# Zero products, a bias add and a float32 inverse in the opening phase of a Fourier and MoE kernel

## The chip, the cores and the metric

The kernel runs on one core of a Trainium2 chip. The metric is the device time of one execution in microseconds (us). The core has five engines that each run their own list of instructions: PE (TensorE, matrix products into the banks of PSUM), DVE (VectorE), ACT (ScalarE), POOL (GpSimd) and SP (SyncE, which here only issues transfers). Transfers (DMAs) are issued from the queues of SP, ACT and POOL. An instruction that waits holds up all that stands behind it on its engine, and the order on each engine is fixed when the program is built: a planner goes through the program in the order in which it is written, weighs it with its own table of costs, and writes one list for each engine.

## The reference

```python
B, S, D, FF = 8, 3008, 256, 2048
X = np.fft.rfft(x, axis=1)                 # x: [8, 3008, 256]
Yr = X.real @ w_r - X.imag @ w_i + b_r     # complex 256x256 product on each bin
Yi = X.real @ w_i + X.imag @ w_r + b_i
Yr, Yi = shrink(Yr, 0.01), shrink(Yi, 0.01)   # sign(y) * max(|y| - 0.01, 0)
y = np.fft.irfft(Yr + 1j * Yi, n=3008, axis=1)
h = np.maximum(y.reshape(24064, 256) @ w_in, 0.0)   # w_in: [256, 2048], float64
out = (h * h) @ w_out                               # w_out: [2048, 256], float64
```

## The kernel before

A Fourier transform of length 3008 = 64 x 47 is done in two stages of matrix products with constant matrices, forward and back. Between them lies the complex product on each bin, the bias and the shrinking. The result goes into the MoE part: two large products with a squared Relu between, which is most of the work.

The 8 batches run one behind the other, and the forward and inverse Fourier work of a later batch is woven into the MoE steps of an earlier one, by jobs with due times in half steps (`jobs`, L755 to L791). The first batch has nothing to be woven into. So the kernel opens with a *front* phase of its own (L653 to L731), with its own SBUF tiles and all eight PSUM banks, and then a *main* phase.

**The ring.** `Fwd32` (L370 to L392) is the first Fourier stage of batch 0. Seven loads of x (tag `big`, four buffers) come in on SP's queue. DVE folds each into a sum and a difference (L380, tag `small`, four buffers), PE multiplies them with `am32` (L384), ACT evicts to `xe` (L391), SP's queue stores to the scratch tensor `s1`. In the loop at L666 the load of a later x is issued ahead of a tile's product, and both ahead of the store of the one before. At the start `load_bias` (L128) loads the bias and a selector matrix on ACT's queue, into two of the four `small` buffers; ACT and DVE turn them into `bb` and `one`.

**Second-batch tiles.** `Fwd2` (L348) is the same stage for the thirteen tiles of batch 1, with four float32 products each instead of folds. With `PRE, FILL = 10, 3`, three of them run after the ring, seven after the units, and the last three in the main phase. In the front their evictions go to tag `xf`, two buffers, and their stores to POOL's queue.

**The units.** `Unit32` (L405 to L452) takes one of the 24 groups of bins of batch 0 through the second Fourier stage (`fwd`, L422), a sign change (`bins`, L428), the product with the weights (`mix`: one product `one` x `bb` for the bias at L433, then four with `w32` at L437), the shrinking (`shrink`: ACT's Relu from the bank at L442, DVE's minimum at L443) and the first inverse stage (`back`, L449). `store_back` (L252) splits the result into a high and a low part (`kuh` by ACT, `kul` by DVE) and stores both to the scratch `s3` on SP's queue. The loop at L703 runs `fwd` and `bins` for unit r+1, `shrink` for r-1, `back` and the store for r-2, and `mix` for r. The matrices of four units at a time (`kbb`, `kk`) are loaded by `load_group`, behind the store of an earlier unit.

**The weights.** The MoE weights come as float64, in 16 parts. `convert` (L689) puts a part together from its two 32-bit halves: five or six DVE passes and one on ACT, then a split into a high and a low part in the reduced float32 format of PE (`fp32r`), and for `w_in` the sums of a Strassen-like scheme. Ten parts are converted between the units, one for every two; parts 10 to 12 behind the units; parts 13, 14, 15 in the main phase at half steps 1, 3 and 5 (`LATER`).

**The second inverse stage.** `Back` (L462 to L500) reads `s3` into `du` and multiplies it with `dx_sb` in three `fp32r` products for each half of the channels (L484, L487, L488), sixteen *Backs* for a batch; ACT and DVE add the two columns of results (L489, L494) into `yr`. `Tokens` (L509) then splits `yr` for the MoE products, and `Step` (L545) runs them: `psh` with the sums on DVE, Relu, square and cast on ACT, a subtraction on POOL, and `pso`. At L740 the first tile's loads, products and splits are issued in this order.

Of the kernel before, what the change touches and what calls it, by code (L numbers as in the profile page):

```python
# [35 lines left out]
    "w320": 1, "w321": 1, "big": 4, "small": 4, "ds": 1, "dw": 3, "ka": 4, "xe": 7, "sel": 1, "bb": 1,  # L36
    "kv": 3, "psf": 8, "x6": 7, "xf": 2, "nam": 1,
# [21 lines left out]
def fnet_moe(ctx: ExitStack, tc, x, w_r, w_i, b2, w_in, w_out, bm, cm, dx, a32, c32, sel, out):  # L59
# [7 lines left out]
    s3 = [dram.tile([M2 + M2, NP, D], F32, name=f"s3_{b}") for b in range(B)]  # L67
# [7 lines left out]
    low = const.tile([128, 1], F32, name="low")  # L75

# [34 lines left out]
    w32 = []  # L111

    def load_mix_weights():
        for j, w in enumerate((w_r, w_i)):
            st = T(f"w32{j}", [128, 2, D], F32)
            w32.append(st)
            act.dma_start(st, w.rearrange("(c p) d -> p c d", p=128))

# [8 lines left out]

    def load_bias():  # L128
        bf = T("bf", [34, D], F32, tag="small")
        sf = T("sf", [34, 128], F32, tag="small")  # L130
        act.dma_start(bf, b2)
        act.dma_start(sf, sel)
        bb = T("bb", [34, D], F32R)
        one = T("sel", [34, 128], F32R)
        copy(act, one, sf)
        copy(act, bb, bf)
        sub(dve, bb[32:], bf[32:], bb[32:])
        return one, bb
# [74 lines left out]
    class Fwd:  # L213
# [4 lines left out]
        def load(self):  # L218
            self.xt = T("xt", [M1, 1, 2, D], F32)
            load_next(self.xt, x[self.b, :M1, self.q:self.q + 1])  # L220
# [31 lines left out]
    def store_back(b, g, ps, eng):  # L252
        uh = T("kuh", [128, D], F32R)
        ul = T("kul", [128, D], F32R)
        done = copy(act, uh, ps)
        if eng is None:
            sub(dve, ul, ps, uh)
        else:
            u = T("ku", [128, D], F32)
            done = copy(act, u, ps)  # L260
            sub(eng, ul, u, uh)
        rows = s3[b].rearrange("m p c -> (m p) c")
        for v, m in ((uh, 4 * g), (ul, 128 + 4 * g if 4 * g < 64 else 32 + 4 * g)):
            put = nc.sync.dma_start(rows[m * NP:m * NP + 128], v.bitcast(F32))
        return done, put


    class Pair:
# [70 lines left out]
        def back(self, g):  # L339
# [5 lines left out]
            store_back(self.b, self.g + g, ps[:, :D], None)  # L345


    class Fwd2(Fwd):  # L348
# [8 lines left out]
        def run(self):  # L357
# [12 lines left out]
    class Fwd32(Fwd):  # L370
        def load(self):
            self.xt = T("x4", [128, 2, 2, D], F32, tag="big")
# [22 lines left out]

    def load_group(k, after, eng=nc.sync):
        group[k] = []
        for name, src in (("kbb", bm), ("kk", c32)):
            t = T(name, [128, 4, 128], F32)
            with tc.issue_after(after.ins):  # L400
                after = eng.dma_start(t, src[:, 4 * k:4 * k + 4])
            group[k].append(t)
        return after

    class Unit32:  # L405
        def __init__(self, b, g):
            self.b, self.g = b, g

        def load(self):
            if self.g % 2 == 0:  # L410
                self.pair = T("ka", [128, 2, D], F32)
# [3 lines left out]
            else:  # L415
                self.pair = units[self.g - 1].pair
            self.a = self.pair[:, self.g % 2]

        def fwd(self):
            self.ps = ps = bank([128, 2, 256])  # L420
            for c in range(2):
                nc.tensor.matmul(  # L422
                    ps[:, c, 0:128], self.a[:, c * 128:(c + 1) * 128], group[self.g // 4][0][:, self.g % 4], start=True, stop=True
                )

        def bins(self):
            self.x = T("kx", [128, 2, 192], F32)
# [3 lines left out]
        def mix(self):  # L431
            self.ps = ps = bank([128, 512])
            nc.tensor.matmul(ps[:, :D], one, bb, start=True, stop=False)  # L433
            for n in range(4):
                j, c = divmod(n, 2)
                js = slice(64, 192) if j == 0 else slice(0, 128)
                nc.tensor.matmul(ps[:, :D], self.x[:, c, js], w32[j][:, c], start=False, stop=n == 3)  # L437

        def shrink(self):
            self.v = v = T("kv", [128, D], F32)  # L440
            r = T("kr", [128, D], F32)
            act.activation(r, self.ps[:, :D], AF.Relu, bias=low)  # L442
            self.cut = dve.scalar_tensor_tensor(  # L443
                out=v, in0=self.ps[:, :D], scalar=LAM, in1=r, op0=ALU.add, op1=ALU.min
            )

        def back(self):
            self.ps = ps = bank([128, 512])
            nc.tensor.matmul(ps[:, :D], group[self.g // 4][1][:, self.g % 4], self.v, start=True, stop=True)  # L449

        def store(self):
            self.done, self.put = store_back(self.b, self.g, self.ps[:, :D], None)  # L452
# [9 lines left out]
    class Back:  # L462
# [8 lines left out]
        def load(self):  # L471
            self.u = T("du", [128, 3, D], F32R, tag="du" if self.spans[0][0] else "mc")
            ps = slice(2 * self.q, 2 * self.q + 2)
            load_next(self.u[:, :2].bitcast(F32), s3[self.b][:128, ps])
# [3 lines left out]
        def mm(self):  # L478
            self.y = y = T("dy", [128, 2, W2], F32)
# [176 lines left out]
    PRE, FILL = 10, 3  # L656
    second = [Fwd2(1, q) for q in range(J)]

    act.dma_start(am32, a32)
    dve.memset(low, -LAM)  # L660
    for f in ring[:FRONT["big"]]:
        f.load()
    nam = T("nam", [M1, M1], F32)
    act.mul(nam, am32[:, 1], -1.0)
    one, bb = load_bias()
    for r in range(len(ring) + 1):  # L666
        if r:
            at(ring, r - 1 + FRONT["big"], "load")
        at(ring, r, "mm")
        at(ring, r - 1, "put")  # L670
        if r == 1:
            with tc.issue_after(ring[0].done.ins):
# [212 lines left out]
```

## Time and profile before

| | |
|---|---|
| median of 3 runs | 2627.17 us (2626.59 to 2628.38) |
| profiled execution | 2630.95 us, of which 2629.2 are span |
| PE busy over the span | 2583.0 us |
| DVE, ACT, POOL busy | 1777.3, 1679.2, 1630.6 us |
| first ring product | 5.61 us |
| first unit's product | 33.89 us |
| last unit's inverse product | 116.79 us |
| MoE steps in a row from | 147.72 us |

The profile's span runs from the first to the last instruction of one execution. In lists of instructions and of groups each row names the engine, the line, the operation, and the tiles it writes and reads (out<-in); behind the bar or in brackets stands the idle time of the engine ahead of it and what ended it. The chain of waits is read from its end: each piece is what released the piece that follows. A float32 product appears as two matmuls (two passes), an `fp32r` product as one. PEclk is the clock granted to TensorE as a share of full speed. A line number can be that of a helper (L98 copies, L102 subtracts).

### The profile page before, as it was taken

The numbers are of one execution on the slowest core, as the hardware profiler recorded it, in microseconds if no ns is written. First come the engines' busy times: TensorE is split into PE (matmuls) and PEld (weight loads), VectorE is DVE, ScalarE is ACT, GpSimd is POOL, SyncE is SP. The second block draws the span as 40 slices with busy tenths as digits, with TensorE's granted clock in tenths as the row PEclk, the third lists the DMA queues.
The fourth block names the chain that finished last, engine by engine and source line by source line (L and its number), as shares of the span: only waits on it lengthen the run. The fifth ranks groups of instructions, "written<-read, shape, count | busy, mean of one in ns | idle before, by whom it ended". The sixth has DMA issues, their size and how long they took to land.

```text
span 2629.2 us, 47506 instructions
## 1 busy us (share of the span) xinstructions
PE 2583.0 (98%) x16932; PEld 2352.2 (89%) x16932; DVE 1777.3 (68%) x3773; ACT 1679.2 (64%) x2445; POOL 1630.6 (62%) x1607
## 2 busy tenths in 40 slices
PE   8979999999999999999999999999999999999999
PEld 5769989999999999999999999999999999999998
DVE  4787766676766667677675766767667677765554
ACT  4556656666666666666666666666666666666665
POOL 0046656766676667666675676666766666666564
PEclk9989999999999999999999999999999999999999
DMA  8723333233332333223332333223332223221100
GB/s 270 247 90 91 109 95 104 87 104 93 113 90 83 108 102 95 88 85 104 103 95 87 101 101 104 90 83 99 102 108 87 72 80 94 75 69 36 37 16 16
DMA packets 190782, 250.63 MB, mean 95 GB/s; under 512 B 21592, under 2 KB 135828, under 8 KB 190548
## 3 DMA queue, kind: packets, MB, share of 16 engines
q1 hardware_dynamic: 176469, 221.71, 27.1%
q0 software_dynamic: 13040, 24.68, 3.7%
q8 instruction: 136, 2.23, 0.4%
q10 hardware_dynamic: 1039, 1.22, 0.1%
q14 instruction: 98, 0.80, 0.1%
HBM read 146.98 MB, written 100.53 MB: 94 GB/s over the span
## 4 chain that ended last, share of the span: by engine, by line
PE 93%; DMA 3%; DVE 2%; POOL 1%; issue 1%; ACT 0%; SPq 0%; ACTq 0%; POOLq 0%; DVEq 0%
PE pso L507 39%; PE psh L507 35%; PE psf L310 7%; PE psf L289 3%; PE psf L245 2%; PE psf L342 2%; PE psf L437 1%; PE psf L487 1%; PE psf L488 1%; PE psf L484 1%; DMA du<-s 1%; DMA s<-xe 1%; DMA kbb<-bm_in 1%; PE psf L422 0%; DMA sf<-sel_in 0%
## 5 line engine op out<-in xcount | busy, mean ns | idle before, releaser
L102 POOL TENSOR_TENSOR mg<-mc,mg 128x500 fp32r<-128x500 f32 (+1 forms) x768 | 975.8, 1291 | 593.1 <-ACT mg L98 560.5
L507 PE MATMUL pso<-mg,wout 128*128 128x500 f32 (+1 forms) x4608 | 1179.4, 393 | 1.4 <-ACT mg L98 1.3
L507 PE MATMUL psh<-yt,win 128*128 128x250 f32 (+1 forms) x8064 | 1071.6, 281 | 9.7 <-DVE mc L507 8.1
L507 ACT ACTIVATE mc<-mc 128x1000 f32<-128x1000 f32 (+1 forms) x768 | 802.7, 1045 | 411.8 <-DVE mc L507 403.0
L507 PEld LDWEIGHTS psh<-yt,win 128*128 128x128 f32 x8064 | 1022.0, 189 | 41.9 <-issue 7.5
L507 PEld LDWEIGHTS pso<-mg,wout 128*128 128x128 f32 x4608 | 819.3, 189 | 132.5 <-POOL mg L102 2.4
L507 DVE TENSOR_TENSOR mc<-psh,mv 128x500 f32<-128x500 f32 (+3 forms) x768 | 419.5, 548 | 430.9 <-PE psh L507 398.1
L98 ACT CAST mg<-mc 128x1000 fp32r<-128x1000 f32 (+1 forms) x384 | 396.9, 1033 | 18.7 <-ACT mc L507 0.4
L507 DVE TENSOR_TENSOR mv<-psh,mu 128x500 f32<-128x500 f32 (+1 forms) x384 | 260.8, 679 | 52.9 <-PE psh L507 21.4
L310 PE MATMUL psf<-wx,kxh 128*128 128x256 f32 x1008 | 207.5, 283 | 1.7 <-ACT xe L98 0.7
L99 DVE COPY mp<-psh 128x250 f32<-128x250 f32 (+1 forms) x384 | 159.9, 416 | 34.3 <-PE psh L507 11.2
L310 PEld LDWEIGHTS psf<-wx,kxh 128*128 128x128 f32 x1008 | 166.8, 189 | 6.4 <-ACT xe L98 0.9
L102 POOL TENSOR_TENSOR ksl<-kv,ksh 128x512 fp32r<-128x512 f32 x84 | 108.8, 1295 | 96.5 <-ACT ksh L98 96.4
L507 DVE TENSOR_TENSOR mu<-psh,mp 128x250 f32<-128x250 f32 (+1 forms) x384 | 160.7, 419 | 11.6
L507 DVE TENSOR_TENSOR mc<-psh,mp 128x250 f32<-128x250 f32 (+1 forms) x384 | 157.2, 409 | 4.3 <-PE psh L507 2.8
L224 POOL TENSOR_TENSOR xs<-xt 120x256 f32<-120x256 f32 x156 | 114.7, 755 | 72.9 <-DMA xt<-x_in 67.1
L331 DVE TENSOR_TENSOR kv<-psf,ke 64x256 f32<-64x256 f32 x336 | 141.8, 422 | 19.9 <-PE psf L310 12.0
L310 PE MATMUL psf<-wx,kxl 128*128 128x256 f32 x504 | 141.7, 281 | 1.9 <-DVE kxl L102 1.9
L98 ACT COPY dy<-psf 128x188 f32<-128x188 f32 x256 | 76.8, 312 | 85.2 <-PE psf L488 84.6
L322 DVE TENSOR_TENSOR ke<-psf,bias 128x512 f32<-128x512 f32 x84 | 58.1, 692 | 101.0 <-PE psf L310 100.7
L98 ACT CAST ksh<-kv 128x512 fp32r<-128x512 f32 x84 | 52.0, 620 | 115.0 <-DVE kv L102 114.2
L494 DVE TENSOR_TENSOR yr<-psf,dy 128x188 f32<-128x188 f32 (+4 forms) x256 | 78.2, 313 | 68.1 <-ACT dy L98 61.6
(103 smaller groups left out, 2548.7 us busy)
## 6 DMA issues: line engine op xcount, KB each, us to landing
du<-s SPq DMA_DIRECT2D x128, 256.0 KB, 2.8
ka<-s SPq DMA_DIRECT2D x96, 256.0 KB, 3.4
s<-kuh SPq DMA_DIRECT2D x192, 128.0 KB, 1.7
s<-kul SPq DMA_DIRECT2D x192, 128.0 KB, 1.8
kcm<-cm_in POOLq DMA_DIRECT2D x84, 256.0 KB, 3.3
s<-xe SPq DMA_DIRECT2D x82, 240.0 KB, 2.4
xt<-x_in SPq DMA_DIRECT2D x81, 240.0 KB, 3.6
du<-s SPq DMA_DIRECT2D x256, 64.0 KB, 2.8
```

The lines of the kernel that those rows point to most:

```text
L98: return act.copy(out=out, in_=in_)
L99: return eng.tensor_copy(out=out, in_=in_)
L102: return eng.tensor_tensor(out=out, in0=a, in1=b, op=ALU.subtract)
L224: return eng.tensor_tensor(out=out[:, :n], in0=self.xt[:, :n, 0], in1=self.xt[:, :n, 1], op=(ALU.add, ALU.subtract)[t])
L245: nc.tensor.matmul(ps[:M1, t], am32[:, t], self.u[:, t], start=True, stop=True)
L289: nc.tensor.matmul(pv[:, :, c, g, :], self.a[:, g, c * 128:(c + 1) * 128], bg, start=True, stop=True)
L310: self.last = nc.tensor.matmul(ps, l, wx[j][:, k, c, :], start=n == 0, stop=n == 5)
L322: dve.tensor_add(out=self.e, in0=self.pe, in1=bias)
L331: dve.tensor_add(out=v[64 * r:64 * r + 64, g], in0=ps[gs], in1=self.e[gs, r])
L342: nc.tensor.matmul(ps[:, :D], self.cm[:, g, j * 128:(j + 1) * 128], r[:, g], start=n == 0, stop=n == 2)
L494: self.cut = dve.tensor_add(out=o, in0=ps[:, 0, lo:hi], in1=y[:, c, lo:hi])
L507: last_of[eng] = op(*args, **kwargs)
```

## The change

- `load_bias`, its selector input and the bias product are gone. The bias is loaded into `b32`, one half of the partitions for each of its two rows, and DVE adds it to the bank before Relu; Relu and the minimum then read SBUF.
- A tile `warm` is set to zero, and three float32 products of it, 512 columns each, stand ahead of the ring on PE.
- The ring has a fifth x buffer (`x5`); the load of a later x now follows the product in the loop; the first three loads of batch 1 stand right behind the ring's loads.
- Batch 0's inverse is in float32: a unit stores one float32 tile `y` (evicted by ACT) instead of two, and `Back` for batch 0 makes four float32 products of 94 columns with `dx32` (K = 96) and one eviction by ACT (`mm32`).
- Four second-batch tiles instead of seven stand behind the units, with the last unit's product ahead of them, evicted to the seven `xe` buffers; tiles 7 to 9 run in the main phase behind the first tile's inverse products, evicted to a buffer of `mg0`; tiles 10 to 12 run later as jobs.
- Conversions: parts 10 and 11 behind the units, parts 12 to 15 at half steps 1, 5, 9 and 11. Some due times of batch 1's jobs move by half a step or so. The units' tiles are allocated with their loads.

```diff
 def load_mix_weights():
+        for st, w in zip(w32, (w_r, w_i)):
             act.dma_start(st, w.rearrange("(c p) d -> p c d", p=128))
+        for j in range(2):
+            act.dma_start(b32[64 * j:64 * j + 64, :], b2[j:j + 1].broadcast_to([64, D]))
...
 class Fwd2: def run
-            self.ev = T("xe", [M1, 1, 2, D], F32, tag="xe" if self.q >= PRE else "xf")
+            self.ev = T("xe", [M1, 1, 2, D], F32, tag="mg0" if PRE <= self.q < EDGE else "xe")
-            self.store(nc.sync if self.q >= PRE else pool)
+            self.store(nc.sync if self.q >= EDGE else pool)
...
 class Unit32: def mix
-            nc.tensor.matmul(ps[:, :D], one, bb, start=True, stop=False)
...
         def shrink(self):
-            act.activation(r, self.ps[:, :D], AF.Relu, bias=low)
-            self.cut = dve.scalar_tensor_tensor(
-                out=v, in0=self.ps[:, :D], scalar=LAM, in1=r, op0=ALU.add, op1=ALU.min
-            )
+            v, r = self.v, self.r
+            dve.tensor_add(out=v, in0=self.ps[:, :D], in1=b32)
+            act.activation(r, v, AF.Relu, bias=low)
+            self.cut = dve.scalar_tensor_tensor(out=v, in0=v, scalar=LAM, in1=r, op0=ALU.add, op1=ALU.min)
...
         def store(self):
-            self.done, self.put = store_back(self.b, self.g, self.ps[:, :D], None)
+            self.done = copy(act, self.y, self.ps[:, :D])
+            m = 4 * self.g * NP
+            self.put = nc.sync.dma_start(s3[self.b].rearrange("m p c -> (m p) c")[m:m + 128], self.y)
...
 class Back
+        def mm32(self):
+            ps = bank([128, 512])[:, :2 * W2].rearrange("c (k p t) -> c k p t", k=2, p=2)
+            for c in range(2):
+                for p in range(2):
+                    self.last = nc.tensor.matmul(
+                        ps[:, c, p], self.u[:, p, c * 128:c * 128 + 128], dx32, start=True, stop=True
+                    )
+            for n, (t, lo, hi, at) in enumerate(self.spans):
+                if t not in raw:
+                    raw[t] = T("yr", [128, 2, 2 * HM], F32)
+                if n:
+                    self.y = T("dy", [128, 2, W2], F32)
+                o = self.y[:, :, lo:hi] if n else raw[t][:, :, at:at + hi - lo]
+                self.done = copy(act, o, ps.rearrange("c k p t -> c k (p t)")[:, :, lo:hi])
...
-    PRE, FILL = 10, 3
+    PRE, FILL, EDGE = 7, 3, 10
...
+    warm = T("warm", [128, 512], F32, tag="small")
+    dve.memset(warm, 0.0)
+    ps = bank([128, 512])
+    for n in range(3):
+        nc.tensor.matmul(ps, warm[:, :128], warm, start=True, stop=True)
     for r in range(len(ring) + 1):
-        if r:
-            at(ring, r - 1 + FRONT["big"], "load")
         at(ring, r, "mm")
+        if r < 2:
+            at(ring, r + FRONT["big"] + 1, "load")
         at(ring, r - 1, "put")
...
-    LATER = {1: 13, 3: 14, 5: 15}
+    LATER = {1: 12, 5: 13, 9: 14, 11: 15}
...
     for q in range(FILL, PRE):
+        with tc.issue_after(units[-1].mm.ins):
-        second[q].run()
+            second[q].run()
...
     for n in range(len(parts) - LATE, min(LATER.values())):
+        convert(n, units[-1], units[-1])
+    for job in first[1]:
+        job()
+    for q in range(PRE, EDGE):
+        with tc.issue_after(first[1][-1].__self__.last.ins):
+            second[q].run()
+    for job in first[2]:
+        job()
```

More of the change, by code (lines that the diff above doesn't have):

```diff
@@ L58, in fnet_moe @@
 @with_exitstack
-def fnet_moe(ctx: ExitStack, tc, x, w_r, w_i, b2, w_in, w_out, bm, cm, dx, a32, c32, sel, out):
+def fnet_moe(ctx: ExitStack, tc, x, w_r, w_i, b2, w_in, w_out, bm, cm, dx, a32, c32, d32, out):
     nc = tc.nc
@@ L126, in split_mix_weights @@
             sub(dve, wx[1][:, j], w, wx[0][:, j])
[L128 to L138, printed above, removed]
     class Double:
@@ L762, in fnet_moe @@
                 if b == 0:
-                    first, step, end = 11.2, 5.3, 9.1
-                    for q in range(PRE, J):
-                        if q > PRE + 1:
-                            jobs += [(0.9 * (q - PRE - 2), second[q].load)]
-                        jobs += [(0.5 + 0.9 * (q - PRE), second[q].run)]
+                    first, step, end = 11.8, 5.25, 9.1
+                    for q in range(EDGE, J):
+                        jobs += [(0.9 * (q - EDGE), second[q].load)]
+                        jobs += [(2.3 + 0.9 * (q - EDGE), second[q].run)]
                     jobs += [(first - 0.6, pairs[1][0].load)]
@@ L872 @@
         "c32_in": cm.transpose(1, 0, 2).astype(np.float32),
-        "sel_in": sel,
+        "d32_in": dm.astype(np.float32),
     }
```

122 lines of the change are left out of this document (62 added, 60 removed).

## The prediction

> **What bounds the kernel now.** I read the page first, then the busy times of each engine by stretches, the chain of waits up to 180 us, the timeline around each idle stretch of PE, and the groups of instructions of the stages. The page's head:
>
> ```profile
> span 2629.2 us, 47506 instructions
> ...
> PE 2583.0 (98%) x16932; PEld 2352.2 (89%) x16932; DVE 1777.3 (68%) x3773; ACT 1679.2 (64%) x2445; POOL 1630.6 (62%) x1607
> ```
>
> The profiled execution took 2630.95 us, of which 2629.2 are span; the median of the runs is 2627.17, 3.8 lower. I sum against 2630.95 and take 3.8 off at the end. TensorE bounds the whole, but the diff touches the first 180 us, where it does not. The view of stretches (columns: busy us of PE, PEld, DVE, ACT, POOL with their counts, granted PE clock, DMA share, GB/s):
>
> ```profile
> 8.00:12.00 4.00, 4.00 (x6) 0.88 (x4) 1.62 (x4) 1.32 (x4) 0.00 (x0) 1.00 0.59 209
> 20.00:24.00 4.00, 1.09 (x4) 0.65 (x4) 2.77 (x6) 2.48 (x6) 0.00 (x0) 1.00 0.97 378
> 24.00:28.00 4.00, 3.33 (x8) 2.63 (x9) 1.09 (x2) 0.20 (x1) 0.00 (x0) 0.58 0.95 349
> 28.00:32.00 4.00, 3.73 (x17) 2.83 (x16) 0.00 (x0) 1.17 (x2) 1.09 (x2) 1.00 0.50 158
> 34.00:44.00 10.00, 10.00 (x37) 7.75 (x37) 0.76 (x2) 2.34 (x9) 0.00 (x0) 0.66 0.98 343
> 44.00:111.00 67.00, 63.46 (x302) 48.76 (x301) 54.86 (x121) 37.91 (x104) 0.00 (x0) 1.00 0.79 243
> 126.70:137.50 10.80, 4.47 (x20) 3.46 (x18) 0.03 (x1) 2.72 (x7) 2.12 (x4) 0.83 0.72 239
> 147.70:177.20 29.50, 20.22 (x135) 18.27 (x135) 29.11 (x53) 17.33 (x27) 15.37 (x12) 0.90 0.32 95
> 180.00:230.00 50.00, 49.96 (x327) 45.55 (x326) 37.40 (x73) 29.96 (x42) 30.09 (x27) 0.98 0.26 77
> ```
>
> There are four stages. Up to 34 us the transfers decide (shares 0.95 and more, with two holes of 0.59 and 0.50). From 44 to 111, the 24 units of the first batch, PE decides. From 117 to 177 it is a change of hands: in 126.7 to 137.5 DVE does nothing (0.03 us) and PE half, then DVE is full (29.11 of 29.50) and PE waits. From 180 on PE is full: whatever reaches that state earlier ends earlier by as much, and whatever adds PE work behind it ends later by as much.
>
> **The change part by part.**
>
> *Ring and zeros (0 to 34 us).* The front's timeline and chain:
>
> ```profile
> 5.61 6.58 PE L384 MATMUL psf<-x,am 120*120 120x512 f32 x8 [5.61 <-DVE x L380]
> ...
> 11.89 4.31 DVE L380 TENSOR_TENSOR x<-x 120x512 f32<-120x512 f32 x7 [0.88 <-ACT sel L98]
> ...
> 12.63 7.13 PE L384 MATMUL psf<-x,am 120*120 120x512 f32 x16 [0.45 <-DVE x L380]
> ```
> ```profile
> 1.70 9.83 DMA sf<-sel_in
> ...
> 13.21 7.26 DMA x<-x_in
> ...
> 23.68 6.77 DMA s<-xe
> ...
> 30.54 3.22 DMA ka<-s
> ```
>
> The first 8 matmul passes take 6.58/8 = 0.82 us, the later ones 7.13/16 = 0.45, so PE runs at half rate until about 12.6. Gone are the bias's two loads, two ACT copies and a DVE subtraction; the selector's load (9.83) held back ACT and, behind it, the folds at 11.89. A fifth x buffer and loads issued ahead of the stores let x stream; today the last load leaves at 13.21 and lands at 20.5. The zeros are 3 products of 512 columns, 6 passes, 6 x 0.82 = 4.9 us from about 1.6 to 6.5, so they may hold the first ring product (5.61) for 0.9 us; transfers hide that, because PE is not last here. If they were, the 0.9 would count. New on ACT's queue are two bias broadcasts and the float32 inverse matrix; they stand behind the group loads, ahead of no work of the ring.
>
> What can be won is idle transfer time: (1-0.59) x 4 = 1.6 us around 10, and of (1-0.50) x 4 = 2.0 around 30 (the last store landing) a part. I take 3. From below 0, if the same bytes only move in another order; from above 6, about what the x loads come earlier (20.5 against 13 to 14 when nothing holds them).
>
> After the ring, PE is done with the three early second-batch tiles and waits for *ka*. Rows 20:24 and 24:28 show that after 1.09 us of work in 4 the clock is 0.58, and 34:44 shows the units begin at 0.66. The zeros lie 20 us before that, so I count nothing for the units' start; were it kept at full clock, it would be (1-0.66) x 10 = 3.4 us more. The Trainium skill ("TensorE: Matmul & The Clock Gate", section "HAM oscillation — how this bites in real kernels") has it that idle gaps of PE longer than about 3.4 us bring half rate back; by that rule too three products at the start cannot reach the units, and a sum in which they did would be 3.4 lower.
>
> *Units (34 to 117 us).* One unit in the chain, and the groups of the stage:
>
> ```profile
> 103.70 0.44 PE psf L422 x4
> 104.15 0.43 PE psf L449 x2
> 104.58 0.31 PE psf L433
> 104.89 1.92 PE psf L437 x8
> 106.81 0.45 PE psf L422 x4
> ```
> ```profile
> L422 PE MATMUL psf<-kbb,ka 128*128 128x128 f32 x96 | 16.3, 297 | 5.7 <-DMA kbb<-bm_in 3.5 <-DMA ka<-s 2.2
> L443 DVE SCALAR_TENSOR_TENSOR kv<-psf,kr 128x256 f32<-128x256 f32 x24 | 10.2, 423 | 26.8 <-ACT kr L442 26.7
> L102 DVE TENSOR_TENSOR kul<-psf,kuh 128x256 fp32r<-128x256 f32 x23 | 9.7, 420 | 2.2 <-ACT kuh L98 2.2
> L442 ACT ACTIVATE kr<-psf,low 128x256 f32<-128x256 f32 x24 | 11.4, 473 | 22.5 <-PE psf L437 20.7 <-DVE dw L172 1.8
> ```
>
> A unit takes 106.81-103.70 = 3.11 us of PE. The bias product leaves: 0.31, so 2.80 remain, if PE stays the bound: 24 x 0.31 = 7.4. On DVE a 128x256 add comes (not in the trace; bounds are L443 and L102, 0.42 both) and the *kul* subtraction (0.42) goes: no change in work. ACT keeps its four operations. One store of 128 KB instead of two per unit, and *put* no longer waits for DVE; the groups' loads, released by *put*, leave a little earlier while their deadline, two units later, shrinks by 0.6. I leave their 3.5 us of PE waits as they are, give or take 3.
>
> But the chain of a unit is longer: product, add on DVE, Relu on ACT (0.47), minimum on DVE, whereas before Relu read the bank itself. DVE runs its instructions in the order they are written into the program, so between add and minimum it idles unless a weight conversion stands there. Row 44:111: DVE 54.86 us in 67/3.11 = 21.5 units, 2.55 per unit. If it idled through the whole 0.47 and its hand-over each time, about 0.5, the unit would take 3.05 and the gain would be 24 x 0.06 = 1.4; with the gap always filled, 7.4. Conversions are plentiful (ten in this stage) but their pieces depend on each other, so I take 2.9 a unit: 24 x 0.21 = 5. Ends: 0 and 9 (with the stores' bytes gone and the *kbb* waits smaller).
>
> *Change of hands (117 to 180 us).*
>
> ```profile
> 116.79 0.70 PE psf L449 x2
> 117.49 1.74 PE psf L361 x8
> ...
> 127.42 7.59 DMA s<-xe
> ```
> ```profile
> 135.75 0.53 PE L484 MATMUL psf<-dx_sb,du 128*128 128x188 f32 x1 [6.17 <-ACT xe L98]
> ...
> 137.51 0.61 DVE L494 TENSOR_TENSOR yr<-psf,dy 128x188 f32<-128x188 f32 x2 [10.79 <-ACT dy L98]
> ...
> 147.72 2.13 PE L507 MATMUL psh<-yt,win 128*128 128x252 f32 x16 [0.52 <-DVE yt L102]
> ...
> 177.24 1.62 PE L507 MATMUL psh<-yt,win 128*128 128x252 f32 x6 [7.30 <-DVE mc L507]
> ```
> ```profile
> du<-s SPq DMA_DIRECT2D x3, 256.0 KB, 4.8
> ...
> s<-kul SPq DMA_DIRECT2D x2, 128.0 KB, 2.6
> ```
>
> The last unit's product is at 116.8 to 117.5, the first tile's steps run from 147.7: 30 us. Seven second-batch tiles sit between, with two *xf* buffers, so their eviction waits for stores of up to 7.59 us and holds ACT, the banks and the first inverse product until 135.75. After the change four tiles go there (with *xe*'s 7 buffers no eviction waits for a store), the inverse products next, then three more tiles while DVE splits the tokens. Worked out from the last unit's end: a tile's 8 passes take 1.74, four tiles 7; the put's landing (2.6) and the *du* load (up to 4.8) are some 7 to 8 with the eviction and run beside them; three inverse products 3; token splits 5 (142 to 147.7 now, with pieces of a conversion between). Steps begin at 16 instead of 30: 14 us, less two tiles that now come later, 2 x 1.74 = 3.5: 10.5. The stores of the late tiles go by POOL's queue, idle then.
>
> DVE sets a limit beside this: from 117 to 177 it has only the idle 10.8 us and the eviction adds of three inverse products (12 adds of about 0.3, 3.6 us), which go, together 14.4. The four last conversions move from steps 0 to 2 to steps 0, 2, 4 and 5, so the 7.30 us stall at 177 is spread; each is still ready before its use (parts 12 and 13 before step 6, parts 14 and 15 before the outputs of steps 6 and 7). That gives at best 4 more. Against it, a faster unit stage leaves some conversion work over, 24 x 0.21 = 5 us less room of which I charge 2.5. I take 12; ends 6 (DVE late again) and 20 (10.5 + all of 9.3, the part of 147.7 to 177.2 in which PE is idle).
>
> *Inverse stage of batch 0 in float32.*
>
> ```profile
> 151.06 0.27 PE L484 MATMUL psf<-dx_sb,du 128*128 128x188 f32 x1
> 151.18 0.27 PE L487 MATMUL psf<-dx_sb,du 128*128 128x188 f32 x1
> 151.28 0.28 PE L488 MATMUL psf<-dx_sb,du 128*128 128x188 f32 x1
> ```
> ```profile
> 206.43 0.89 PE psf L289 x8
> ```
>
> A *Back* has six passes of 188 columns about 0.11 apart: 0.65. Now it has four float32 products of 94 columns, each two passes: 8 passes; the nearest row, float32 with 128 columns, takes 0.89/8 = 0.11 each, so 0.6 to 0.9. Thirteen of the sixteen lie where PE is full. I take +0.23 each, 3 us lost; ends 0 and, with the 0.2 that a product of another type cost in a unit (L433: 0.31, where the 188-column passes above are 0.11 apart) on both sides, 13 x 0.65 = 8. DVE's adds and a copy disappear; where PE is full that is worth nothing.
>
> *Sum.* 3 + 5 + 12 - 3 = 17. 2630.95 - 17 = 2614, less 3.8: **2610 us**.
>
> **The rivals.**
>
> *DVE becomes the bound of the units.* It idles through every Relu; conversions slide behind the units. For: DVE already waited 26.7 us for *kr*, in order. Against: a filled queue of conversions. Units gain 1.4, the change of hands 2.5 less: 2616.
>
> *The wait at the change of hands only moves.* Main's banks and buffers wait for the front's last evictions and stores, as ACT does now. For: the 6.17 us row. Against: seven buffers. Of 12 remain 2: 2620.
>
> *The zeros do not wake the clock, or the transfers need as long.* Front 0: 2613.
>
> *Slower: the unit's chain through DVE and ACT.* Relu queues behind ACT's long casts, DVE stands before the minimum, PE waits for *back*. With waits of w per unit the pitch is 2.55 + w; over the 20 units with conversions it outweighs the other terms (3 + 12 - 3 = 12) when 20 x (2.55 + w - 3.11) exceeds 12, w above 1.16. With 1.5 us each: 19 lost, 7 net, 2634. For: each engine's order is fixed before the run. Against: *kr*'s measured wait leads to 0.5, and there is more than one unit of slack between *shrink* and *back*.
>
> **How the numbers follow.** About 0.2% (5 us) is what a measurement of this kernel tells from no change. Forecast 0.68, DVE-bound units 0.12, moved wait 0.10, no front gain 0.05, slower 0.05. The forecast's own terms run 0 to 6, 0 to 9, 6 to 20 and -8 to 0; taken together, not all at an end at once, 5 to 31 saved: 2596 to 2622, which holds the second, third and fourth case too. Faster needs below 2621.9: nearly all of the first, second and fourth and two thirds of the third, 0.90; same 0.06; slower 0.04.
>
> **What would show it.** Right: passes of L384's successor at 0.45 us from the first or second ring tile on; *ka* landing by 31; a pitch of 2.8 to 3.0 between units; no wait of ACT for *s<-xe* after the units; the first full run of *psh* about 16 us behind the last *back*; no PE gap of 7 us at step 2. Wrong: a pitch of 3.1 with DVE waiting for *kr*; the first inverse product more than 12 us after the last unit; *psh* still waiting for *mc* over 10 us in sum; float32 *Back* passes that spread to 0.2 us each.

## The result and the profile after

| | before | changed |
|---|---|---|
| median of the runs | 2627.28 us | 2611.98 us (2611.33 to 2612.91) |
| ratio, 95% interval | | 0.9942 [0.9924, 0.9959] |
| profiled execution (span) | 2630.95 us (2629.2) | 2611.79 us (2610.0) |
| first unit's product | 33.89 | 32.60 |
| end of the last unit's inverse product | 117.49 | 109.35 |
| MoE steps in a row from | 147.72 | 131.38 |

The change makes the kernel 15.3 us faster; 2610 was forecast. The two profiled executions differ by 19.2 us, because the one of before lay 3.7 above its median (2627.28, now of four runs) and this one 0.2 below. The table splits the 19.2 into 1.3 at the front, 6.8 over the units (83.6 to 76.8 us), 8.2 between the units and the steps (30.2 to 22.0) and 2.9 from there to the end.

The page's head, of the changed kernel:

```profile
span 2610.0 us, 47374 instructions
...
PE 2572.4 (99%) x16946; PEld 2351.9 (90%) x16946; DVE 1761.2 (67%) x3731; ACT 1675.6 (64%) x2432; POOL 1628.4 (62%) x1607
```

The stretches of the changed kernel (columns as in the prediction):

```profile
12.00:20.00 8.00, 6.19 (x16) 2.66 (x15) 4.24 (x8) 3.08 (x7) 0.00 (x0) 1.00 1.05 324
28.00:36.00 8.00, 3.40 (x12) 3.16 (x13) 0.00 (x0) 1.10 (x4) 0.00 (x0) 0.50 0.85 262
36.00:108.00 72.00, 62.87 (x321) 54.92 (x321) 59.70 (x132) 41.54 (x113) 0.00 (x0) 0.99 0.66 212
160.00:170.00 10.00, 7.03 (x45) 5.74 (x44) 9.76 (x17) 6.70 (x8) 7.89 (x7) 1.00 0.01 2
170.00:180.00 10.00, 7.48 (x40) 6.36 (x39) 10.00 (x17) 5.75 (x7) 4.87 (x4) 0.90 0.00 0
240.00:260.00 20.00, 16.98 (x108) 15.58 (x107) 13.03 (x27) 9.25 (x15) 13.62 (x15) 0.91 0.41 117
131.38:2610.00 2478.62, 2463.41 (x16469) 2266.18 (x16467) 1677.43 (x3555) 1611.54 (x2272) 1622.35 (x1592) 1.00 0.29 86
```

The last row is set against the same stretch of before, from its own first run of steps:

```profile
147.72:2629.20 2481.48, 2459.34 (x16425) 2261.78 (x16425) 1689.59 (x3584) 1611.18 (x2278) 1623.99 (x1591) 1.00 0.29 87
```

Behind the start of the steps PE has 4.1 us more work (2463.41 against 2459.34), and it idles 15.2 us instead of 22.1. More than half of the idle time that is left lies in three stretches above: 160 to 180, where DVE is full (9.76 and 10.00 of 10) and PE does 7.03 and 7.48, and 240 to 260, where PE does 16.98 of 20.

The timeline of the changed kernel, PE and ACT, at the landmarks (start, duration; in brackets the idle time ahead and what ended it):

```profile
6.74 9.01 PE L365 MATMUL psf<-x,am 120*120 120x512 f32 x20
16.92 2.54 ACT L99 COPY xe<-psf 120x512 f32<-120x512 f32 x5 [7.42 <-DMA w<-w_r_in]
32.60 2.05 PE L409 MATMUL psf<-kbb,ka 128*128 128x128 f32 x8 [7.02 <-DMA ka<-s]
108.01 1.34 PE L433 MATMUL psf<-kv,kk 128*128 128x256 f32 x4 [1.74 <-DVE kv L429]
124.86 0.40 ACT L99 CAST yt<-yr 128x252 fp32r<-128x252 f32 x1 [4.65 <-DMA s<-xe]
131.38 2.22 PE L515 MATMUL psh<-yt,win 128*128 128x252 f32 x16
```

Three of these rows carry a wait that the forecast's sum did not have. At 16.92 ACT stood 7.42 us behind its own weight loads with ring evictions queued. At 108.01 PE waited for DVE's *kv*, and did so five times in the units. At 124.86 the first token split waited 4.65 us for a store to land. The first and the third of them are taken away in experiments below.

### The profile page after: what moved, and what is told of

Read it like the earlier page. It is cut to its first block, busy times and chain, and to the rows that moved or that the text cites. A ratio compares the mean times of both kernels' runs of the same rounds, so it can differ in the third digit from the quotient of the medians.

```text
span 2610.0 us, 47374 instructions
## 1 busy us (share of the span) xinstructions
PE 2572.4 (99%) x16946; PEld 2351.9 (90%) x16946; DVE 1761.2 (67%) x3731; ACT 1675.6 (64%) x2432; POOL 1628.4 (62%) x1607
## 4 chain that ended last, share of the span: by engine, by line
PE 93%; DVE 2%; DMA 2%; POOL 1%; issue 1%; ACT 1%; SPq 0%; POOLq 0%; ACTq 0%; DVEq 0%
PE pso L515 39%; PE psh L515 35%; PE psf L291 7%; PE psf L270 3%; PE psf L232 2%; PE psf L323 2%; PE psf L495 1%; PE psf L496 1%; PE psf L492 1%; PE psf L423 1%; PE psf L342 1%; DMA s<-xe 1%; DMA du<-s 1%; POOL mg L103 1%; DMA kbb<-bm_in 0%
## 5 line engine op out<-in xcount | busy, mean ns | idle before, releaser
L99 ACT COPY dy<-psf 128x188 f32<-128x188 f32 (+2 forms) x229 | 68.5, 313 | 66.2 <-PE psf L496 65.8
L103 POOL TENSOR_TENSOR yt<-ms,yt 128x500 fp32r<-128x500 f32 (+1 forms) x94 | 108.2, 1152 | 2.5 <-ACT yt L99 2.3
```

Source lines behind the costliest of these rows:

```text
L99: return act.copy(out=out, in_=in_)
L103: return eng.tensor_tensor(out=out, in0=a, in1=b, op=ALU.subtract)
```

## The experiments

Each is the changed kernel with one edit, except in the last group, where the changed kernel stands once without an edit and two edits are also put together. Ratios are to the kernel before on the same chip; the changed kernel itself was timed again in the last group.

### Terms of the sum, undone one by one

**No zeros.**

```diff
-    warm = T("warm", [128, 512], F32, tag="small")
-    dve.memset(warm, 0.0)
-    ps = bank([128, 512])
-    for n in range(3):
-        nc.tensor.matmul(ps, warm[:, :128], warm, start=True, stop=True)
```

> The changed kernel without the three products of zeros. My theory: the ring's products then run at half rate for some us more, but ACT (held 7.42 us behind its own weight loads) and the transfers decide when the last ring store lands, so the first unit's product stays at 32.6 +/- 0.7 and the time at 2612 +/- 1.5. Rival (the zeros carry the front's gain): the ring ends 3 us or more later, the first unit's product comes at 35 or later, the time is 2615 or more.

Measured 2611.63 us, ratio 0.9935 [0.9917, 0.9953]; the first unit starts at 33.06. The zeros do wake the clock: without them the first ring passes are these,

```profile
5.82 4.62 PE L365 MATMUL psf<-x,am 120*120 120x512 f32 x5 [5.82 <-DVE x L361]
```

0.92 us a pass against 9.01/20 = 0.45 with them. The half rate is read from the passes here: the granted clock says 1.00 from 6 to 12 us in both kernels. The gain is 0.5 us at the first unit and none that can be seen at the end, since PE is not last in this stage.

**Bias back on PE.**

```diff
+            nc.tensor.matmul(ps[:, :D], one, bb, start=True, stop=False)
...
-            dve.tensor_add(out=v, in0=self.ps[:, :D], in1=b32)
-            act.activation(r, v, AF.Relu, bias=low)
+            act.activation(r, self.ps[:, :D], AF.Relu, bias=low)
```

> The changed kernel with the bias as a product on PE again (selector and split bias loaded as before, Relu and minimum read the bank), all else as changed. My theory: the clear pitch of a unit goes from 2.61 back to 3.11, and DVE loses one add per unit, so that its waits shrink; the last unit's inverse product comes 4 to 8 us later and the time is 2616 to 2620. Rival (DVE already bounds the units of the changed kernel, the product was free): last inverse product within 2 us of 108.0, time 2612 to 2614.

Measured 2616.36 us, 0.9947 [0.9933, 0.9962], 4.7 above the kernel without zeros of the same group. The two intervals overlap and the runs just touch (2614.29 to 2616.79 against 2610.45 to 2614.71), so the size is rough. The units' stretch:

```profile
36.00:108.00 72.00, 72.00 (x338) 56.44 (x337) 53.66 (x107) 40.32 (x112) 0.00 (x0) 0.98 0.65 209
```

PE is full again and sets the pitch, which is 3.11 us as before (two bias products in a row start at 61.48 and 64.59); the changed kernel has 62.87 of 72. The last unit ends at 111.76, 2.4 later than in the changed kernel, less than the 4 to 8 that I expected; the rest of the 4.7 comes behind it.

**Batch 0's inverse split again.** Units store a high and a low part, and the *Backs* of batch 0 make three `fp32r` products for each half.

```diff
-            self.done = copy(act, self.y, self.ps[:, :D])
-            m = 4 * self.g * NP
-            self.put = nc.sync.dma_start(s3[self.b].rearrange("m p c -> (m p) c")[m:m + 128], self.y)
+            self.done, self.put = store_back(self.b, self.g, self.ps[:, :D])
...
-            if self.b == 0:
-                return self.mm32()
```

> The changed kernel with batch 0's inverse in fp32r again: units store a high and a low part, Back makes six fp32r products and DVE adds. My theory: PE gets back 13 x 0.25 = 3 us behind 180 us, but each unit has a DVE subtraction of 0.42 and a second store again while DVE already makes PE wait, and the change of hands has 12 more DVE adds: units 3 to 6 us longer, time 2611 to 2617. Rival (the float32 products cost PE 0.6 or more each): 2604 to 2608.

Measured 2624.10 us, 0.9986 [0.9975, 0.9996]: undoing this part gives back most of the gain, more than either theory had. The profiled execution is the lowest of its runs (2619.45), 7.7 above that of the changed kernel; the median is 12.5 above the kernel without zeros. Its stretches, and then its DVE groups in the units (busy us, mean ns):

```profile
36.00:108.00 72.00, 62.61 (x312) 54.37 (x312) 62.37 (x147) 39.38 (x109) 0.00 (x0) 0.97 0.76 245
360.00:380.00 20.00, 16.19 (x95) 14.43 (x96) 12.68 (x26) 6.70 (x14) 9.59 (x12) 0.91 0.38 117
```
```profile
L427 DVE TENSOR_TENSOR kv<-psf,b 128x256 f32<-128x256 f32 x22 | 9.2, 420 | 14.8 <-PE psf L423 14.7
L103 DVE TENSOR_TENSOR kul<-psf,kuh 128x256 fp32r<-128x256 f32 x21 | 8.8, 420 | 2.2 <-ACT kuh L99 2.0
```

DVE now carries the bias (9.2) and the low parts (8.8) together, and the last unit ends at 113.78 instead of 109.35. The steps start at 134.84, 3.5 later than in the changed kernel. Another 4.6 us go at 300 to 700, nearly all in the stretch shown, which is full in the changed kernel; before loses time at the same place (15.90 of 20). So the float32 inverse is worth some 8 to 12 us; it is no loss of 3. Its price on PE was as forecast; what it takes off DVE in the units was not in this term, because the prediction had set it against the bias add. The stall at 360 to 380 is in both programs with the split inverse and in none of the others. Whether it comes from the *Back* additions on DVE or from another order of the woven jobs, which the planner makes anew for every program, these runs do not separate.

**Seven tiles behind the units, two eviction buffers.**

```diff
-    PRE, FILL, EDGE = 7, 3, 10
+    PRE, FILL, EDGE = 10, 3, 10
...
-            self.ev = T("xe", [M1, 1, 2, D], F32, tag="mg0" if PRE <= self.q < EDGE else "xe")
+            self.ev = T("xe", [M1, 1, 2, D], F32, tag="xe" if self.q >= PRE else "xf")
```

> The changed kernel with seven second-batch tiles behind the units and two eviction buffers for them, as before. My theory: ACT waits for these stores again (some 8 us), the first full run of token products starts 8 to 12 us later than at 131.4, and the time is 2618 to 2622. Rival (DVE's backlog decides, the earlier start only moves the wait): time 2612 to 2615 though the run starts later.

Measured 2621.93 us, 0.9971 [0.9959, 0.9983], 10.3 above the kernel without zeros. The first inverse product and the steps in its timeline:

```profile
129.27 5.44 PE L473 MATMUL psf<-dx,du 96*128 96x94 f32 x24 [6.24 <-ACT xe L99]
...
142.07 2.20 PE L515 MATMUL psh<-yt,win 128*128 128x252 f32 x16
```

The 6.17 us wait that the prediction quoted from before is back as 6.24, and the steps start 10.7 later. This part of the change is what I said it was. The edit undoes the number of tiles and the number of buffers together; which of them counts for how much is not separated.

### The new waits, taken away one by one

**Weight and group loads behind the ring, on SP's queue.**

```diff
-            act.dma_start(st, w.rearrange("(c p) d -> p c d", p=128))
+            nc.sync.dma_start(st, w.rearrange("(c p) d -> p c d", p=128))
...
-            with tc.issue_after(ring[0].done.ins):
-                load_mix_weights()
-                last = load_group(0, ring[0].done, act)
-                with tc.issue_after(last.ins):
-                    act.dma_start(dx32, d32)
+    with tc.issue_after(ring[-1].last.ins):
+        load_mix_weights()
+        last = load_group(0, ring[-1].last)
+        nc.sync.dma_start(dx32, d32)
```

> The changed kernel with the mixing weights, the bias, the first group's matrices and the float32 inverse matrix loaded on SP's queue behind the last ring store, instead of on ACT's queue behind the first ring eviction, where ACT stood for 7.42 us. My theory: the bytes bound the opening (transfer share 0.9 to 1.06 from 4 to 28 us), so the wait of ACT goes and the first unit's product still comes at 32.6 +/- 1; time 2610 to 2613. Rival (ACT's wait delays the ring stores and so the units): ACT has no wait over 2 us in the ring, the first unit's product comes at 28 to 30.5, the time is 2607 to 2610.

Measured 2605.20 us, 0.9909 [0.9894, 0.9924]. My theory, that the bytes bound the front, fell. ACT's queue in the changed kernel (start, duration) and then two rows of this one:

```profile
8.92 0.58 ACT L99 COPY xe<-psf 120x512 f32<-120x512 f32 x1 [0.27 <-PE psf L365]
8.92 0.43 ACTq L114 DMA_DIRECT2D w<-w_r_in  x1
10.63 0.37 ACTq L114 DMA_DIRECT2D w<-w_i_in  x1
...
13.86 0.36 ACTq L383 DMA_DIRECT2D kbb<-bm_in  x1
15.17 0.35 ACTq L383 DMA_DIRECT2D kk<-c_in  x1
16.55 0.33 ACTq L696 DMA_DIRECT2D dx<-d_in  x1
```
```profile
28.67 2.05 PE L409 MATMUL psf<-kbb,ka 128*128 128x128 f32 x8 [5.44 <-DMA ka<-s]
...
28.00:36.00 8.00, 7.33 (x30) 6.64 (x31) 1.43 (x4) 2.05 (x7) 0.00 (x0) 0.62 1.05 402
```

In the changed kernel ACT goes from one issue to the next in 0.9 to 1.7 us (the two bias loads, left out above, are the quick ones) while the transfer engines are at 1.05 of their share, and no eviction runs between. In the kernel before, ACT's four load issues in the ring were 0.5 us apart, from 11.57 to 13.05, with the engines at 0.68. With the loads behind the ring, ACT's evictions follow one another without that hole, the stretch from 28 to 36 moves 402 GB/s instead of 262, and the units begin 3.9 us earlier (28.67 against 32.60). Why an issue takes that long was not tested; that these issues hold up what is behind them on ACT was. The edit moves the loads to another queue and to a later place at once, and what the place alone is worth was not separated.

**Evictions that leave the token buffers alone.** The first token tile lies in memory over three of the front's eviction buffers, so its first write waits for their stores.

```diff
-            self.ev = T("xe", [M1, 1, 2, D], F32, tag="mg0" if PRE <= self.q < EDGE else "xe")
+            self.ev = T("xe", [M1, 1, 2, D], F32, tag="mg1" if self.q == EDGE - 1 else "mg0" if PRE <= self.q < EDGE else "x6" if FILL <= self.q < PRE else "xe")
```

> The changed kernel with the evictions of second-batch tiles 3 to 6 in used-up x6 buffers and that of tile 9 in the second mg1 buffer: the first token split no longer stands on memory that a store still reads (4.65 us of ACT at 124.9, 4.12 us at 134). My theory: the first full run of token products starts at 126 to 128 instead of 131.4, and since DVE is full from 148 on and has 7 us less idle before, 2 to 5 us reach the end: 2607 to 2610. Rival (DVE's conversions decide alone, or other buffers are late next): the run starts earlier by less than 2, or the time is 2611 to 2613 all the same.

Measured 2605.12 us, 0.9907 [0.9892, 0.9921]. The first split and the steps in its timeline:

```profile
119.60 0.40 ACT L99 CAST yt<-yr 128x252 fp32r<-128x252 f32 x1
...
125.83 2.20 PE L515 MATMUL psh<-yt,win 128*128 128x252 f32 x16
```

The 4.65 us wait is gone, and the steps start 16.7 us after the last unit's end (109.11), where the prediction had 16. The same edit gives tile 9 another buffer, and with it goes a wait of ACT of 4.12 us for a store at 133.96; how the gain splits between the two was not measured.

**Zeros in the gap ahead of the units.**

```diff
     for q in range(FILL):
         second[q].run()
+    ps = bank([128, 512])
+    for n in range(7):
+        nc.tensor.matmul(ps, warm[:, :128], warm, start=True, stop=True)
```

> The changed kernel with seven more products of zeros on PE between the early second-batch tiles and the units, where PE waits 7.0 us for ka at a granted clock of 0.50. My theory of the clock: the units then start at full rate, the first 4 units take 2 to 3 us less, the last inverse product comes 1 to 3 us earlier, time 2609 to 2611. Rival (the units' start is bounded by their loads and conversions, or zeros do not hold the clock): the last inverse product stays within 1 us of 108.0 and the time within 1.5 us of 2612.

Measured 2610.49 us, 0.9926 [0.991, 0.9943]. The stretch, and PE's waits up to the end of the units (us in all, times, longest):

```profile
28.00:36.00 8.00, 7.99 (x30) 4.63 (x29) 0.00 (x0) 1.16 (x5) 0.53 (x1) 1.00 0.90 264
```
```profile
PE psf L433 <- DVE kv L429: 4.5, 5, 1.7
PE psf L409 <- DMA kbb<-bm_in: 4.1, 2, 2.0
```

The granted clock is 1.00, against 0.50 in the changed kernel, so the zeros work where the gap is and not 20 us ahead of it, as the prediction had it. The 3.4 us that it put on this came in part and did not reach the end. The first unit starts 0.7 us later, behind the zeros, but the first inverse product comes at 38.86 instead of 40.52, 1.7 us ahead. Of these, 0.3 go in the first wait for *kbb*, and 0.9 between 76 and 88 us, where the clock granted in this execution is 0.82 and then 0.90, against 1.00 in the changed kernel. The last unit ends at 109.02, 0.3 us before that of the changed kernel, and the medians do not tell the two kernels apart. The waits shown are in sum no longer than the changed kernel's (5.5 and 3.7). The Trainium skill ("TensorE: Matmul & The Clock Gate", section "HAM oscillation — how this bites in real kernels") has half rate follow idle gaps of more than about 3.4 us; the 7.02 us gap with its 0.50 and the filled one with 1.00 agree, while the dip to 0.82 stands behind a gap of 2.02 us only.

**Part 12 converted behind the units, parts 13 to 15 left late.**

```diff
-    LATER = {1: 12, 5: 13, 9: 14, 11: 15}
+    LATER = {5: 13, 9: 14, 11: 15}
```

> The changed kernel with weight part 12 converted behind the units (with parts 10 and 11) instead of at half step 1. My theory: its 3 us of DVE work fall into the 7.2 us in which DVE idles before the first token split, so PE's waits for DVE between 148 and 178 (5.5 us) shrink: 2608 to 2611. Rival (its pieces stand ahead of the token splits in DVE's order): the first full run of token products starts 2 us or more later than 131.4 and the time is 2612 to 2615.

Measured 2612.96 us, 0.9937 [0.9922, 0.9952]: the ratio of the changed kernel (0.9942). By itself the place of part 12 is worth nothing.

### What adds up, and the conversions

**The changed kernel again**, with no edit, as the measure for the three that follow.

> The changed kernel once more, beside the three that follow, so that their differences are taken on one chip. Every theory expects 2610 to 2613, by the ratio to the kernel before 0.993 to 0.995.

Measured 2610.71 us, 0.9939 [0.9925, 0.9953], span 2608.4, steps from 131.00.

**Both waits taken away** (the loads behind the ring, and the evictions off the token buffers; the two diffs together).

> The changed kernel with both edits that helped: the opening's weight loads on SP behind the last ring store, and the late evictions in buffers that the first token split does not need. Theory (two waits one behind the other, at different places): the gains add, 6.8 + 6.9, 2597 to 2600. Rival (both only move the start of one stretch that DVE's conversions end): 2602 to 2605.

Measured 2603.06 us, 0.9909 [0.9896, 0.9923], the lowest median of all, but in ratio no better than either edit alone (0.9909 and 0.9907); the time is the rival's, not my theory's. The steps start at 121.88, 9.1 us before the changed kernel's, so the two gains nearly add there (4.6 and 5.5 alone); the span is only 7.2 shorter. What is lost lies behind: PE's two short stretches are as in the changed kernel,

```profile
150.00:160.00 10.00, 7.01 (x44) 5.73 (x43) 9.76 (x17) 6.43 (x9) 8.01 (x7) 1.00 0.00 0
160.00:170.00 10.00, 7.43 (x44) 6.60 (x44) 10.00 (x17) 5.50 (x8) 5.63 (x4) 0.93 0.01 2
```

DVE full and PE at 7, ten us earlier than in the changed kernel. From the start of the steps to the end PE has 1.4 us more work than there and 0.5 more idle time: with an earlier start more of the second batch's tiles fall behind it.

**Low halves on POOL in the units.** On top of the last: the subtractions that split the first ten weight parts go from DVE to POOL, which is idle there.

```diff
-            p.split()
+            p.split(pool if n < 10 else dve)
...
-            win_sums(n // 4, parts[n - 1:n + 1])
+            win_sums(n // 4, parts[n - 1:n + 1], pool if n < 10 else dve)
```

> The kernel with both edits, and with the low halves of the weight parts converted between the units subtracted by POOL, idle there, instead of DVE (0.4 us of DVE less per unit). Theory A (DVE's load bounds the units, 2.55 a unit against a clear pitch of 2.61): PE's waits for kv (5.5 us) shrink, the last inverse product comes 2 to 5 us earlier than in the kernel with both edits, and 1 to 4 us reach the end. Theory B (DVE and POOL hinder each other, as DVE's pass of 0.68 us between the units takes up to 1.65 beside POOL's work behind 135 us): DVE passes between the units stretch over 1 us and the last inverse product comes within 1 us of that kernel's or later.

Measured 2605.37 us, 0.9916 [0.9902, 0.9929]. From the first unit to the last one's end it takes 79.5 us, where the kernel with both waits taken away takes 76.9. DVE's groups from 30 to 108 us, first with both waits taken away, then with the halves on POOL:

```profile
L429 DVE SCALAR_TENSOR_TENSOR kv<-kv,kr 128x256 f32<-128x256 f32 x24 | 10.1, 421 | 1.0 <-ACT kr L428 0.9
L427 DVE TENSOR_TENSOR kv<-psf,b 128x256 f32<-128x256 f32 x24 | 10.0, 418 | 7.2 <-PE psf L423 7.2
```
```profile
L429 DVE SCALAR_TENSOR_TENSOR kv<-kv,kr 128x256 f32<-128x256 f32 x24 | 14.8, 615 | 4.1 <-ACT kr L428 4.0
L427 DVE TENSOR_TENSOR kv<-psf,b 128x256 f32<-128x256 f32 x24 | 10.0, 417 | 10.2 <-PE psf L423 10.2
```

The minimum (L429), with both inputs in SBUF, goes from 421 to 615 ns while POOL works; the bias add (L427), with one input in PSUM, stays at 417. Instruction by instruction, five of these minima overlap a subtraction on POOL and take 1.36 us on average, the other 19 take 0.42; of the adds five overlap one too, and all take 0.42. Taking work off DVE in this way makes the rest of it slower. The Trainium skill ("SBUF — State Buffer", section "Who interferes with whom") says that a DVE instruction with two SBUF inputs contends with a GpSimd instruction that reads SBUF, and one with at most one SBUF input, outside the two-port modes, does not; these two groups agree. Two other groups show that one SBUF input is no safeguard by itself: the conversion's passes of L145 and L146, with one input, take 0.95 and 0.75 us beside POOL instead of 0.42. Whether they run in such a mode no run here shows.

**Conversions at the old places.** Part 12 behind the units, parts 13 to 15 at half steps 1, 3 and 5.

```diff
-    LATER = {1: 12, 5: 13, 9: 14, 11: 15}
+    LATER = {1: 13, 3: 14, 5: 15}
```

> The changed kernel with the weight parts converted at the old places: part 12 behind the units, 13, 14, 15 at half steps 1, 3 and 5. My theory: PE's single stall in the first steps comes back (7.3 us before, two stalls of 4.2 us in sum now), 3 to 5 us reach the end: 2615 to 2617. Rival (only the sum of DVE's work counts, not its places): 2611 to 2613.

Measured 2604.02 us, 0.9911 [0.9897, 0.9924], 6.7 below the changed kernel of the same group (5.2 in the spans), with the steps from 131.60 against 131.00. The stretches at the old places, and then those of the changed kernel of this group:

```profile
170.00:180.00 10.00, 9.66 (x68) 8.75 (x67) 5.24 (x12) 5.38 (x8) 8.83 (x10) 1.00 0.53 150
240.00:260.00 20.00, 20.00 (x136) 18.40 (x135) 12.14 (x27) 13.38 (x20) 13.12 (x13) 1.00 0.30 88
100.00:500.00 400.00, 391.20 (x2563) 356.69 (x2562) 278.74 (x566) 253.56 (x374) 247.55 (x250) 0.99 0.34 101
```
```profile
170.00:180.00 10.00, 7.48 (x38) 6.43 (x37) 10.00 (x17) 5.89 (x7) 4.38 (x4) 0.85 0.00 0
240.00:260.00 20.00, 16.89 (x107) 15.48 (x106) 12.73 (x26) 9.60 (x16) 13.63 (x15) 0.91 0.41 120
100.00:500.00 400.00, 386.24 (x2522) 352.78 (x2522) 276.31 (x557) 250.91 (x370) 244.08 (x246) 0.99 0.33 100
```

The new places cost 5.0 us of PE between 100 and 500 us: the pile of conversion and sums on DVE ends by 170 instead of 180, and the stall at 244 (PE 2.5 us for ACT's *kxh*) is not there. As early conversion of part 12 alone gave nothing, it is the places of parts 13 to 15 that cost. A stall of 2.7 to 5.1 us between 220 and 260 us is in every run with the new places, also where the steps start earlier, and in neither this one nor the kernel before. What in the new places makes ACT late there was not followed.

The old places together with both waits taken away was not tried; nor were the old places with the zeros in the gap.

## Why the prediction was right, point by point

The total was right to 2 us, and the stages that were to get faster did. Term by term it was less good: errors cancelled. In the profiled executions 1.3 came for 3, 6.8 for 5, and 11.1 (8.2 and 2.9) for the 12 - 3 = 9 of the two last terms, 19.2 for 17. That the total came so near is in part luck, since one term has the wrong sign, and one part of another has too.

- **Ring, 3 forecast, 1.3 measured.** The passes run at 0.45 us from the start as said, and *ka* landed at 32.6, not by 31. The failing sentence is that the new loads on ACT's queue "stand behind the group loads, ahead of no work of the ring". ACT's ring evictions stood 7.42 us behind those loads. Moving them gained 3.9 at the first unit, near the 6 that I gave as the upper end.
- **Zeros, nothing forecast, nothing measured**, at the ring and for the units, and for the reason given.
- **Units, 5 forecast, 6.8 measured.** One unit in the changed kernel's chain of waits:

```profile
45.55 0.44 PE psf L409 x4
46.00 0.43 PE psf L433 x2
46.43 1.73 PE psf L423 x8
48.16 0.46 PE psf L409 x4
```

  The pitch is 48.16-45.55 = 2.61, not 2.80: with the `fp32r` bias product gone (0.31), the float32 products behind it also take 1.73 instead of 1.92. That is 24 x 0.50 = 12 on PE; 5.5 of it went back as waits of PE for *kv*:

```profile
PE psf L433 <- DVE kv L429: 5.5, 5, 1.7
```

  The 5 was near for a partly wrong reason. DVE does take a part back, but not by idling through Relu: in the units its minimum waited 0.7 us for *kr* in all, so the rival built on that idling did not come, nor the slower one. Neither engine is full there: from 46 to 106 us PE and DVE are each busy for 52.5 of 60. The waits come one behind the other (PE, DVE, PE):

```profile
55.10 0.68 PE L409 MATMUL psf<-kbb,ka 128*128 128x128 f32 x4 [1.73 <-DMA kbb<-bm_in]
57.39 1.23 DVE L103 TENSOR_TENSOR win<-ds,win 128x1024 fp32r<-128x1024 f32 x1 [1.95 <-ACT win L99]
59.67 0.70 PE L433 MATMUL psf<-kv,kk 128*128 128x256 f32 x2 [1.28 <-DVE kv L429]
```

  PE waits for the load of *kbb*, so ACT's copy of the bank comes late, and behind it on ACT the cast of *win*; DVE waits for that cast, and *kv* behind it comes late for PE. At 80.55, 82.87 and 85.15 the same three rows stand again. So 2.6 of the 5.5 us begin at a load whose waits I had left as they are. That the add pays on DVE hangs in large part on the float32 inverse, which removes *kul*; I had booked the two as "no change in work", and not as one term that stands only on the other.
- **Change of hands, 12 forecast, 8.2 measured up to the steps' start.** Evictions of the four tiles wait for no store, as said, and seven tiles with two buffers bring the 6.2 us wait back. The steps start 22.0 us behind the units, not 16. The moved wait that I gave 0.10 did come, at one more buffer: the token tile shares memory with the evictions, and its first write waits until their stores have read it. Without that it is 16.7. The other part, "at best 4 more" from spread conversions, had the wrong sign: the new places cost 5 to 7.
- **Float32 inverse, 3 lost forecast.** The price on PE was sized well. Behind the steps' start a *Back*'s eight passes stand as

```profile
145.74 0.86 PE psf L473 x8
```

  against an estimate of 0.6 to 0.9. What failed is the sign of the term: splitting again costs 8 to 12 us, 3.5 of them up to the steps' start. The step at fault is that this term held only PE's price, while the *kul* subtraction that goes was used up in the units' term. "DVE's adds and a copy disappear; where PE is full that is worth nothing" may have failed too, by the 4.6 us between 300 and 700 us, but the cause of these is open.

In short: the float32 inverse and the four tiles with their seven eviction buffers make the gain, the bias on DVE adds some 5, roughly measured, on top of the first, and the zeros add nothing. The new places of the conversions take 5 to 7 away, and the two unnoticed waits 7.6 together, hardly more than either alone.

## What to carry to other kernels

Price an edit on the engine that it relieves as well as on the one it loads: two edits can each look neutral or dear and pay only together. Where a wait is removed, follow the next buffer to the memory that it shares and to the transfers that must land first, and follow each moved transfer to the engine that issues it, because it holds up that engine's own work. Work that is spread to later places is no gain by itself, since it meets other work there.

## What the hardware showed that I had not expected

- Transfers issued by ACT at a DMA share of 1.05 followed one another by 0.9 to 1.7 us, against 0.5 us at a share of 0.68 in the kernel before, and evictions behind them on ACT waited 7.42 us.
- DVE instructions with both inputs in SBUF, and some with one, slow beside a working POOL. The conversion's 0.68 us pass, in the units where POOL is idle and from 135 to 182 us where it works (ns: least, median, most):

```profile
L147 DVE SCALAR_TENSOR_TENSOR df<-da,df x10: 680/683/693, 42.9 to 99.6; 128x512 int32<-128x512 int32 x10
```
```profile
L147 DVE SCALAR_TENSOR_TENSOR df<-da,df x4: 672/1534/1649, 140.5 to 179.7; 128x512 int32<-128x512 int32 x4
```

- One `fp32r` product among float32 ones costs more than its own time: 0.50 us a unit for a product of 0.31, and the 3.11 us pitch came back with it.
- Products of zeros hold the granted clock as others do: 1.00 instead of 0.50.
